# Spreading the attention output over three cycles, moving a layer norm later, and interleaving two MLP output groups in a transformer block

## The chip, the cores and the metric

The kernel runs on one core of one Trainium2 chip. The metric is the device time of one execution in microseconds (us). Times below are medians of two to four runs (seven for the kernel before in the later rounds). One trace was kept of each kernel.

## The reference

A pre-norm block: sliding-window attention (window 256, 32 heads of 32), then an MLP with SiLU, each with a residual.

```python
x = A_x                                       # [1, 2048, 1024] bf16
h  = x + attn(layernorm(x), wqkv, wo)         # 32 heads, key at most 255 positions back
h2 = h + silu(layernorm(h) @ w1) @ w2         # hidden size 3584
```

## The kernel before

The sequence is cut into four blocks of 512 rows. Attention of block `b - 1` runs woven into the projections of block `b`; attention of the last block is woven into the output projection (`wo_group`) of blocks 0 to 2. That weaving goes in cycles: three cycles (kinds A, B, C) for each of 8 head groups.

```python
def scores(b, g, kind):                       # TensorE -> sc[0], sc[1]; ScalarE exp; GpSimd masks
    ...
    for pair in range(2):
        e = e_of(b * G + g, kind, pair)
        nc.scalar.activation(out=e[:, :, lo:hi], in_=sc[pair][:, :, lo:hi], func=ACT.Exp, scale=scale)
        ...

def attn_out(b, g, pair):                     # 24 small matmuls into one bank, then divide
    for qt in range(4):
        for hh in range(2):
            ...
                nc.tensor.matmul(o_ps[:, qt * 2 + hh, 0:VW], lhsT=e_of(i, kind, pair)[...], rhs=v[...], ...)
    nc.vector.reciprocal(out=recip[:], in_=o_ps[:, :, DH:VW])
    nc.vector.tensor_tensor(out=obuf[i % 3][...], in0=o_ps[...], in1=recip[...], op=ALU.mult)

def tail_of(b, g):
    return [lambda: attn_out(b, g, 0), lambda: attn_out(b, g, 1), lambda: attn_transpose(b, g)]

# ---- last attention stage: 24 cycles, n = 0..23
for g in range(G):
    for kind in KINDS:
        scores(NB - 1, g, kind)
        b, j, c = dense[n]
        if c == 0:
            ... load_res(nb, nj, x2d)          # residual rows for the tile after this one, 256 KB
        wo_group(b, j, c)                      # 8 matmuls; VectorE adds the residual; h to DRAM
        if pending:
            pending.pop(0)()                   # a step of the tail of the head group before
        if n % 2 == 0 and n // 2 < KT:
            nc.sync.dma_start(out=w1[:, n // 2, :], ...)       # 0.9 MB
        if n == 9:
            steps = ln2_steps(0)               # load h of block 0 (1 MB), 4x statistics, 1x root,
        if n == 17:                            # 4x normalise, 4x transpose by DMA
            nc.sync.dma_start(out=w2[0], ...)
        if steps and n >= 9:
            steps.pop(0)()
        n += 1
    pending = tail_of(NB - 1, g)
```

All these transfers are issued, in program order, from one queue (SyncE's). The MLP's first group needs all four transposed tiles of LN2 (the layer norm ahead of the MLP).

The softmax here doesn't subtract the row's maximum and nothing guards it: scores larger than these inputs give would overflow.

## Time and profile before

| | kernel before |
|---|---|
| time, median of 3 runs | 720.51 us (720.36 to 721.69) |
| span of the profiled run | 718.4 us |
| TensorE busy | 695.8 us, 97% |
| VectorE, ScalarE, GpSimd busy | 41%, 36%, 24% |

The prediction shows the lines it rests on. This is the same trace cut by stage: start to the third head group; the rest of the first three attention stages; the last stage; the gap ahead of the MLP; the first MLP layer of block 0. Columns: stretch, length, busy time (instructions) of TensorE, weight loads, VectorE, ScalarE, GpSimd, then the granted clock (TensorE's, as a share of full speed), the busy share of the DMA engines and GB/s.

```profile
70.62:243.82 173.20, 169.97 (x1950) 86.68 (x1981) 84.91 (x202) 120.17 (x133) 116.29 (x253) 1.00 0.23 49
243.82:311.42 67.60, 63.49 (x757) 32.42 (x768) 35.64 (x84) 46.59 (x49) 44.89 (x98) 1.00 0.88 260
311.42:312.44 1.02, 0.00 (x1) 0.03 (x1) 0.69 (x1) 0.22 (x1) 1.02 (x4) 1.00 0.37 69
312.44:375.81 63.37, 63.04 (x330) 29.38 (x337) 25.18 (x39) 16.12 (x27) 0.34 (x1) 1.00 0.39 129
```

The last stage differs from the others in its DMA share: 0.88 against 0.23. And the chain of waits, in this stage, leaves TensorE (shortened; columns: start, length, what):

```profile
271.64 6.40 DMA r_a<-h_dram
278.13 1.30 DVE ln_st L153 x2
...
309.13 3.17 DMA r_a<-r_a
```

From the load of h at 271.64 to the first TensorE piece in the chain at 292.47 it runs through VectorE only, and at the end through the DMA transposes into the MLP.

### The profile page before, as it was taken

The numbers are of one execution on the slowest core, as the hardware profiler recorded it, in microseconds if no ns is written. First come the engines' busy times: TensorE is split into PE (matmuls) and PEld (weight loads), VectorE is DVE, ScalarE is ACT, GpSimd is POOL, SyncE is SP. The second block draws the span as 40 slices with busy tenths as digits, with TensorE's granted clock in tenths as the row PEclk, the third lists the DMA queues.
The fourth block names the chain that finished last, engine by engine and source line by source line (L and its number), as shares of the span: only waits on it lengthen the run. The fifth ranks groups of instructions, "written<-read, shape, count | busy, mean of one in ns | idle before, by whom it ended". The sixth has DMA issues, their size and how long they took to land.

```text
span 718.4 us, 12082 instructions
## 1 busy us (share of the span) xinstructions
PE 695.8 (97%) x4920; PEld 330.1 (46%) x5006; DVE 294.2 (41%) x645; ACT 257.1 (36%) x325; POOL 172.9 (24%) x375
## 2 busy tenths in 40 slices
PE   6899999999999998999999999999999999999998
PEld 2444544554455544444444444444444444444443
DVE  7355745743343436634343314325133352234111
ACT  2315556777777776641230003310023200133000
POOL 1004656766776676630000000000000000000000
PEclk9999999999999999999999999999999999999999
DMA  9440133023400388897105140012310032300010
GB/s 312 156 117 9 31 46 96 16 45 47 140 16 17 108 283 287 232 212 278 47 2 160 37 110 0 1 56 63 81 37 0 1 96 58 82 1 0 30 37 22
DMA packets 75112, 60.56 MB, mean 84 GB/s; under 512 B 48944, under 2 KB 59184, under 8 KB 75056
## 3 DMA queue, kind: packets, MB, share of 16 engines
q1 hardware_dynamic: 75056, 59.78, 29.6%
q8 instruction: 39, 0.64, 0.4%
q14 instruction: 17, 0.14, 0.1%
HBM read 39.85 MB, written 8.39 MB: 67 GB/s over the span
## 4 chain that ended last, share of the span: by engine, by line
PE 91%; DMA 3%; DVE 2%; issue 1%; ACT 1%; POOL 1%; SPq 0%; DVEq 0%; POOLq 0%; ACTq 0%
PE hacc L408 18%; PE hacc L450 17%; PE acc L206 16%; PE acc L450 9%; PE acc L408 9%; PE acc L198 8%; PE sc L234 5%; PE o_ps L270 4%; PE acc L216 4%; PE hacc L216 1%; DMA r_w<-in_A_wqkv_dram 1%; DMA r_a<-h_dram 1%; DMA r_a<-in_B_w_dram 1%; DVE ln_st L153 1%; POOL r_e L260 1%
## 5 line engine op out<-in xcount | busy, mean ns | idle before, releaser
L245 ACT ACTIVATE r_e<-sc 128x1024 bf16<-128x1024 f32 (+2 forms) x192 | 175.8, 967 | 80.0 <-PE sc L234 78.9
L260 POOL TENSOR_SCALAR_AFFINE_SELECT r_e<-r_e 128x256 bf16<-128x256 bf16 (+1 forms) x368 | 169.9, 491 | 139.2 <-ACT r_e L245 136.0
L450 PEld LDWEIGHTS <-r_a 128*128 128x128 bf16 x896 | 87.7, 98 | 106.3 <-issue 0.7
L408 PEld LDWEIGHTS <-r_w 128*128 128x128 bf16 x896 | 87.4, 98 | 106.5 <-issue 1.5
L450 PE MATMUL hacc<-r_a 128*128 128x512 bf16 x548 | 121.5, 379 | 0.6
L408 PE MATMUL hacc<-r_e,r_w 128*128 128x512 bf16 x441 | 100.1, 379 | 0.8
L417 ACT ACTIVATE r_n<-hacc 128x512 f32<-128x512 f32 x30 | 17.9, 597 | 179.5 <-PE hacc L408 128.9
L208 DVE CAST r_a<-acc 128x512 bf16<-128x512 f32 x56 | 38.7, 690 | 88.1 <-PE acc L206 88.1
L450 PE MATMUL acc<-r_a 128*128 128x512 bf16 x332 | 73.8, 379 | 0.6 <-DMA r_a<-in_B_w_dram 0.4
L206 PEld LDWEIGHTS <-r_w 128*128 128x128 bf16 x512 | 46.1, 98 | 58.6 <-issue 8.9
L206 PE MATMUL acc<-r_t,r_w 128*128 128x512 bf16 x242 | 58.5, 380 | 1.7 <-issue 1.4
L206 PE MATMUL acc<-r_w 128*128 128x512 bf16 x246 | 57.1, 380 | 0.8 <-issue 0.5
L270 PEld LDWEIGHTS <-r_e 128*128 128x128 bf16 x1440 | 45.6, 96 | 17.6 <-issue 2.7
L216 PE MATMUL acc<-r_o,r_a 128*128 128x512 bf16 x196 | 48.0, 380 | 1.9 <-DVE r_t L218 0.9
L408 PE MATMUL acc<-r_e,r_w 128*128 128x512 bf16 x216 | 49.1, 379 | 0.0
L270 PE MATMUL o_ps<-r_a,r_e 128*128 128x33 bf16 x1440 | 46.2, 178 | 2.1 <-DVE r_n L278 2.1
L234 PE MATMUL sc<-r_a 32*128 32x128 bf16 (+2 forms) x704 | 46.9, 276 | 0.3
L452 DVE SCALAR_TENSOR_TENSOR r_t<-hacc,r_t 128x512 bf16<-128x512 f32 x20 | 13.7, 684 | 61.4 <-PE hacc L450 61.2
L216 PEld LDWEIGHTS <-r_a 128*128 128x128 bf16 x256 | 23.1, 98 | 30.5 <-issue 5.9
L198 PE MATMUL acc<-r_w 128*128 128x512 bf16 x122 | 29.4, 380 | 5.0 <-ACT r_w L179 4.5
L418 DVE SCALAR_TENSOR_TENSOR r_a<-r_n,hacc 128x512 bf16<-128x512 f32 x30 | 20.6, 688 | 33.0 <-ACT r_n L417 33.0
L452 DVE SCALAR_TENSOR_TENSOR r_t<-acc,r_t 128x512 bf16<-128x512 f32 x12 | 8.3, 692 | 59.6 <-PE acc L450 59.6
(58 smaller groups left out, 429.7 us busy)
## 6 DMA issues: line engine op xcount, KB each, us to landing
r_w<-in_B_w_dram SPq DMA_DIRECT2D x8, 896.0 KB, 6.5
r_a<-in_B_w_dram SPq DMA_DIRECT2D x7, 1024.0 KB, 6.7
r_w<-in_A_wqkv_dram SPq DMA_DIRECT2D x6, 1024.0 KB, 11.9
r_o<-in_A_x_dram SPq DMA_DIRECT2D x16, 256.0 KB, 4.6
r_t<-in_A_x_dram SPq DMA_DIRECT2D x16, 256.0 KB, 3.5
h_dram<-r_t SPq DMA_DIRECT2D x16, 256.0 KB, 2.9
r_t<-h_dram SPq DMA_DIRECT2D x16, 256.0 KB, 2.8
out_dram<-r_t SPq DMA_DIRECT2D x32, 128.0 KB, 1.7
```

Source lines behind the costliest of these rows:

```text
L198: nc.tensor.matmul(acc, lhsT=lnT_b[b % 2][:, kt, j * P:(j + 1) * P], rhs=wqkv[:, kt, col0:col0 + 512], start=(kt == 0), stop=(kt == KT - 1))
L206: nc.tensor.matmul(acc, lhsT=wqkv[:, kt, col0:col0 + P], rhs=lnT_b[b % 2][:, kt, :], start=(kt == 0), stop=(kt == KT - 1))
L208: copy(out=(qT, kT)[which][b][:, g, :], in_=acc)
L216: nc.tensor.matmul(acc, lhsT=qT[b][:, g, j * P:(j + 1) * P], rhs=wo[:, g, c * 512:(c + 1) * 512], start=(g == 0), stop=(g == G - 1))
L234: nc.tensor.matmul(sc[hh // 2][:, hh % 2, ch * P:(ch + nq) * P], lhsT=kT[t // 4][r0:r0 + DH, g, (t % 4) * P:(t % 4 + 1) * P], rhs=qT[b][r0 ...
L245: nc.scalar.activation(out=e[:, :, lo:hi], in_=sc[pair][:, :, lo:hi], func=ACT.Exp, scale=scale)
L260: nc.gpsimd.affine_select(out=ap, in_=ap, pattern=[[0, 2], [0, n], [sgn, P]], compare_op=ALU.is_ge if upper else ALU.is_gt, fill=0.0, base ...
L270: nc.tensor.matmul(o_ps[:, qt * 2 + hh, 0:VW], lhsT=e_of(i, kind, pair)[:, hh, ch * P:(ch + 1) * P], rhs=v[:, b * 4 + kt, g * 4 + pair * 2 ...
L408: nc.tensor.matmul(acc, lhsT=w1[:, kt, ft * P:(ft + 1) * P], rhs=ln2T[b][:, kt, :], start=(kt == 0), stop=(kt == KT - 1))
L418: nc.vector.scalar_tensor_tensor(out=gT[:, ft, :], in0=th, scalar=1.0, in1=acc, op0=ALU.add, op1=ALU.mult)
L450: nc.tensor.matmul(acc, lhsT=gT[:, ft, j * P:(j + 1) * P], rhs=w2[ft // 4][:, ft % 4, c * 512:(c + 1) * 512], start=(ft == 0), stop=(ft == ...
L452: nc.vector.scalar_tensor_tensor(out=t_out[j % 2][:, c * 512:(c + 1) * 512], in0=acc, scalar=0.5, in1=t_in[j % 2][:, c * 512:(c + 1) * 512 ...
```

## The change

Its intent: give every cycle some output matmuls, so that ScalarE's exponentials fit in every cycle; begin LN2's VectorE work later, when its load has surely landed; and put more matmuls ahead of the first use of the last slice of w2, the second MLP weight.

```diff
-    o_ps = ps.tile([P, 8, 64], F32, name="o_ps")
-    tp_ps = ps.tile([P, 1024], BF16, name="tp_ps")
+    o_ps = [ps.tile([P, 8, 64], F32, name=f"o_ps{i}") for i in range(2)]
+    tp_ps = o_ps[1][:].rearrange("p a b -> p (a b)").bitcast(BF16)
 ...
-    def attn_out(b, g, pair):
+    def attn_out(b, g, first, last):
+        for n in range(first, last):           # 16 pieces: 8 of pair 0, 8 of pair 1
+            pair, qt, hh = n // 8, n // 2 % 4, n % 2
 ...
+            if n % 8 == 7:
+                attn_norm(i, pair)
 ...
-        return [lambda: attn_out(b, g, 0), lambda: attn_out(b, g, 1), lambda: attn_transpose(b, g)]
+        def end():
+            attn_out(b, g, 11, 16)
+            attn_transpose(b, g)
+        return [lambda: attn_out(b, g, 0, 5), lambda: attn_out(b, g, 5, 11), end]
 ...
             if n == 9:
                 steps = ln2_steps(0)
+                steps.pop(0)()
 ...
-            if steps and n >= 9:
-                steps.pop(0)()
+            for _ in range(2 if n % 3 == 0 else 1):
+                if steps and n >= 14:
+                    steps.pop(0)()
 ...
+            accs = [next_acc(), next_acc()]
+            if b == 0 and j == 0:              # MLP output: 24 + 24 matmuls, then 4 + 4
+                for c in range(2):
+                    mm2(accs[c], j, c, 0, FT - 4)
```

More of the change, by code (lines that the diff above doesn't have):

```diff
@@ L178, in ln_transpose @@
             nc.tensor.transpose(out=tp_ps[:, kt * P:(kt + 1) * P], in_=xt[:, kt * P:(kt + 1) * P], identity=ident[:])
-        copy(out=dst[:, :, j * P:(j + 1) * P], in_=tp_ps[:].rearrange("p (k q) -> p k q", q=P))
+        copy(out=dst[:, :, j * P:(j + 1) * P], in_=tp_ps.rearrange("p (k q) -> p k q", q=P))
     def ln_tiles(tag):
@@ L262, in mask, with attn_norm @@
                                 fill=0.0, base=0, channel_multiplier=-sgn)
-    def attn_out(b, g, pair):
+    def attn_out(b, g, first, last):
         i = b * G + g
-        for qt in range(4):
-            for hh in range(2):
-                chunks = [x for x in CHUNKS[qt] if b * 4 + x[0] >= 0]
-                for n, (kt, kind, ch) in enumerate(chunks):
-                    nc.tensor.matmul(
-                        o_ps[:, qt * 2 + hh, 0:VW],
-                        lhsT=e_of(i, kind, pair)[:, hh, ch * P:(ch + 1) * P],
-                        rhs=v[:, b * 4 + kt, g * 4 + pair * 2 + hh, :],
-                        start=(n == 0), stop=(n == len(chunks) - 1),
-                    )
+        for n in range(first, last):
+            pair, qt, hh = n // 8, n // 2 % 4, n % 2
+            chunks = [x for x in CHUNKS[qt] if b * 4 + x[0] >= 0]
+            for m, (kt, kind, ch) in enumerate(chunks):
+                nc.tensor.matmul(
+                    o_ps[pair][:, qt * 2 + hh, 0:VW],
+                    lhsT=e_of(i, kind, pair)[:, hh, ch * P:(ch + 1) * P],
+                    rhs=v[:, b * 4 + kt, g * 4 + pair * 2 + hh, :],
+                    start=(m == 0), stop=(m == len(chunks) - 1),
+                )
+            if n % 8 == 7:
+                attn_norm(i, pair)
+    def attn_norm(i, pair):
         recip = small.tile([P, 8, 1], F32, name="recip", tag="recip")
-        nc.vector.reciprocal(out=recip[:], in_=o_ps[:, :, DH:VW])
+        nc.vector.reciprocal(out=recip[:], in_=o_ps[pair][:, :, DH:VW])
         nc.vector.tensor_tensor(
             out=obuf[i % 3][:, :, pair * 64:(pair + 1) * 64].rearrange("p t (h d) -> p t h d", d=DH),
-            in0=o_ps[:, :, 0:DH].rearrange("p (t h) d -> p t h d", h=2),
+            in0=o_ps[pair][:, :, 0:DH].rearrange("p (t h) d -> p t h d", h=2),
             in1=recip[:].rearrange("p (t h) o -> p t h o", h=2).to_broadcast([P, 4, 2, DH]), op=ALU.mult,
@@ L443, with mm2 @@
         steps = ln2_steps(b + 1) if b + 1 < NB else []
+        def mm2(acc, j, c, first, last):
+            for ft in range(first, last):
+                nc.tensor.matmul(acc, lhsT=gT[:, ft, j * P:(j + 1) * P], rhs=w2[ft // 4][:, ft % 4, c * 512:(c + 1) * 512],
+                                 start=(ft == 0), stop=(ft == FT - 1))
         for j in range(4):
@@ L446 @@
                 load_res(b, j + 1, h_dram)
+            accs = [next_acc(), next_acc()]
+            if b == 0 and j == 0:
+                for c in range(2):
+                    mm2(accs[c], j, c, 0, FT - 4)
             for c in range(2):
-                acc = next_acc()
-                for ft in range(FT):
-                    nc.tensor.matmul(acc, lhsT=gT[:, ft, j * P:(j + 1) * P], rhs=w2[ft // 4][:, ft % 4, c * 512:(c + 1) * 512],
-                                     start=(ft == 0), stop=(ft == FT - 1))
+                acc = accs[c]
+                mm2(acc, j, c, FT - 4 if b == 0 and j == 0 else 0, FT)
                 nc.vector.scalar_tensor_tensor(out=t_out[j % 2][:, c * 512:(c + 1) * 512], in0=acc, scalar=0.5,
```

## The prediction

> **What bounds the kernel now.** I read the page's engine shares first, then the timeline of TensorE over a few attention cycles, then VectorE and the DMA-issuing queue where TensorE shows idle time.
>
> ```profile
> PE 695.8 (97%) x4920; PEld 330.1 (46%) x5006; DVE 294.2 (41%) x645; ACT 257.1 (36%) x325; POOL 172.9 (24%) x375
> ```
>
> TensorE leaves 22.6 us of the 718.4 us span unbusy, about half of it in the first 12 us. So a gain must come from the few visible gaps or from idling that the modelled matmul ends hide. The attention part (63 to 311 us) is made of cycles: scores of one kind (A, B or C) into two score tiles, one dense group of eight matmuls, then a "tail" step of the head group before: first attention output of head pair 0, then of pair 1, then only a transfer. Three cycles are a triple; a triple takes 8.02 us (A starts at 123.56, 131.58, 139.60). TensorE, then ScalarE:
>
> ```profile
> 121.40 0.40 PE L234 MATMUL sc<-r_a 32*128 32x128 bf16 x8
> 121.73 1.90 PE L198 MATMUL acc<-r_w 128*128 128x512 bf16 x8
> 123.56 0.73 PE L234 MATMUL sc<-r_a 32*128 32x384 bf16 x8
> 124.23 1.90 PE L198 MATMUL acc<-r_w 128*128 128x512 bf16 x7
> 125.97 0.76 PE L270 MATMUL o_ps<-r_a,r_e 128*128 128x33 bf16 x24
> 126.66 0.40 PE L234 MATMUL sc<-r_a 32*128 32x256 bf16 x8
> 126.99 1.90 PE L198 MATMUL acc<-r_w 128*128 128x512 bf16 x8
> 128.73 0.76 PE L270 MATMUL o_ps<-r_a,r_e 128*128 128x33 bf16 x24
> 129.42 0.40 PE L234 MATMUL sc<-r_a 32*128 32x128 bf16 x8
> ```
>
> ```profile
> 121.92 1.94 ACT L245 ACTIVATE r_e<-sc 128x1024 bf16<-128x1024 f32 x2 [0.70 <-PE sc L234]
> 124.38 1.94 ACT L245 ACTIVATE r_e<-sc 128x1024 bf16<-128x1024 f32 x2 [0.52 <-PE sc L234]
> ```
>
> Cycle lengths are uneven: C 2.16 (no output matmuls), A 3.10, B 2.76. ScalarE needs 1.94 us per cycle plus 0.52 until it can begin again, 2.46. In the 2.16 us cycle that does not fit: A's scores start at 123.56, but the second score tile is read until 121.92 + 1.94 = 123.86. A's scores hold TensorE 0.67 (to 124.23), B's and C's 0.33, for the same number of products. The 0.34 us is a wait inside a line that looks busy. So in two cycles of three TensorE bounds, in the third ScalarE.
>
> Then two places where TensorE is seen idle. VectorE stands still for the load of block 0 for the second layer norm (LN2), and the work TensorE needs queues behind:
>
> ```profile
> 278.13 1.29 DVE L153 BATCH_NORM_STATS2 ln_st<-r_a 128x6 f32<-128x512 bf16 x2 [3.62 <-DMA r_a<-h_dram]
> 279.58 0.64 DVE L218 TENSOR_TENSOR r_t<-acc,r_t 128x512 bf16<-128x512 f32 x1
> ```
>
> ```profile
> 280.26 1.89 PE L216 MATMUL acc<-r_o,r_a 128*128 128x512 bf16 x7 [0.88 <-DVE r_t L218]
> 282.87 0.77 PE L270 MATMUL o_ps<-r_a,r_e 128*128 128x33 bf16 x24 [0.72 <-DVE r_n L278]
> ```
>
> With a third wait of 1.42 at 292.5 the two triples from 275.89 take 9.84 and 9.59: 3.4 us over two normal ones. Second, the DMA queue at the end of attention:
>
> ```profile
> 307.81 2.71 SPq L175 DMA_TRANSPOSE r_a<-r_a  x2
> 312.18 0.33 SPq L221 DMA_DIRECT2D h_dram<-r_t  x1
> 312.60 1.23 SPq L286 DMA_TRANSPOSE r_a<-r_n  x1
> ```
>
> The last LN2 transpose issues about 309.1 and lands 3.2 later; the MLP starts at 312.44 after 1.02 us of idling. A transpose holds the issuing queue for 1.2 to 1.3 us, and the queue is in order.
>
> **What the Trainium skill says.** "TensorE: Matmul & The Clock Gate", section "Wait — 56ns, not 53.3ns?": 215.7 ns start to start at 512 columns and a floor near 25 ns however small the matmul. The trace agrees: 8 dense in 1.73 us (216 each); 24 output matmuls in about 0.60 (25 each). "TensorEngine Tiling (Array Packing)", "Key Properties": changing the tiling mode drains the engine. The trace shows about 0.1 us before each set of scores (dense straight into scores 1.83 against 1.73); once per cycle before and after the change. "PSUM — Partial Sum Buffer", "PSUM bank collisions raise a hardware error": two engines must be kept apart by bank. That is why the output matmuls waited for VectorE's division (0.72 above) with one bank. "TensorE: Matmul & The Clock Gate", "HAM oscillation — how this bites in real kernels": gaps over about 3.4 us re-throttle the array to half speed. No gap of the kernel before, after its start, is that long, so its trace shows nothing of it; the first 14 matmuls do run slow (4 in the first 1.5 us).
>
> **Part 1, even spread.** Nothing is removed: the 48 output matmuls of a triple become 15, 18 and 15. The cost of a cycle to TensorE is 0.33 + 1.73 + 0.10 + 0.025 x 15 = 2.53 for A and C, 2.60 for B; a triple 7.66 to 7.68 instead of 8.02. ScalarE's 2.46 fits in each, by 0.07, so the 0.34 goes and nothing takes its place. In block 0's attention (fewer chunks: 9, 13, 14) the C cycle is 2.51 and a triple 7.2 for 7.54, again 0.34. A scores that follow an output-less C cycle before and a full one after: groups 2 to 7 of the first stage (group 1 follows group 0, whose cycles have no tail) and all 8 of three later stages, 30 in all. 30 x 0.34 = **-10.3 us**. Masks on GpSimd take 5.7 us per triple, below 7.68. The second PSUM bank (the old transpose scratch, free after the start) lets pair 1 begin without waiting for pair 0's division; in steady state that wait was already hidden.
>
> **Part 2, later LN2.** The load stays at cycle 9, the statistics begin at cycle 14 instead of 10, over 10 us later; the load took 6.4. The VectorE stall for it goes. But 13 steps are pressed into 10 cycles, two in cycles 15, 18, 21. Playing VectorE forward (residual add 0.6, division pair 0.62, statistics 1.5 per tile; reciprocal root 2.9 at 135.4, 3.9 at 287.3): it falls about 4 us behind by cycle 17 and the add of cycle 18 comes about 0.9 late for the accumulator of cycle 20. So 3.4 saved, 0.9 given back: **-2.5 us**.
>
> **Part 3, the price of lateness.** The 13 steps end in cycle 23, the last, not in 22. In that cycle the queue first gets the attention transpose, which now follows the output's last five pieces in the same cycle and so waits for VectorE's division, and only then the last LN2 transpose. With the last matmul of attention ending at T: division done T + 1.0 (add 0.6, reciprocal and multiply 0.65 after the dense group), attention transpose 1.23, LN2 transpose issues T + 2.3, lands 3.2 to 3.9 later. The MLP needs all four tiles for its first group, so it starts at T + 5.6 to 6.2 instead of T + 1.0: **+4.8 us**. The gap is over 3.4 us, so I add an estimate from the clock page for half-speed restart: 3.4 us of work at half speed costs 1.7, taken at two chances in three: **+1.2 us**.
>
> **Part 4, interleaved first two MLP outputs.** Before, the last four matmuls of the first group wait 0.42 for the last slice of w2. Now 48 matmuls (10.4 us) come ahead of them, and the load takes 5.5: **-0.4 us**. The rest of the MLP is dense on TensorE and untouched.
>
> Sum: 720.5 - 10.3 - 2.5 + 4.8 + 1.2 - 0.4 = 713.3; I take **713.0 us**, 1.0% faster.
>
> **Rivals.** (a) ScalarE takes over as the bound: margin is only 0.07 us per cycle and about zero in the first stage. For it: C to A needs 2.50 measured and gets 2.51 there. Against: where it binds, it costs hundredths. If 0.1 per A is left, 3 us less gain: 716. (b) The end gap does not appear, because the transposes issue earlier than I order them, and VectorE keeps up: 720.5 - 10.3 - 3.4 - 0.4 = 706.4, just short of 2%. Against: the program order at cycle 23 is plain. (c) VectorE becomes the bound in cycles 14 to 21, by more than 0.9: residual loads also queue behind the waiting attention transposes, and one such wait of 2.57 us is in the trace before. It could eat the whole 3.4: 714. (d) Contention lengthens the last transposes; each further us is one us of time.
>
> **Range and chances.** The attention term is well measured (8.5 to 10.5), LN2 0 to 3.4, the gap 3 to 6.5, the clock 0 to 2. Together 708.5 to 717.5. Faster by over 2% needs below 706.1, lower than rival (b): 0.06. Slower by over 2%: 0.01.
>
> **What would show it.** A's scores (384-wide) should hold TensorE 0.33, triples last about 7.7, ScalarE idle before A grow by about 0.1 and before B and C shrink. VectorE's wait for the block 0 load should be gone; a small TensorE wait on the residual add near cycle 20 may be there. Before the first MLP group TensorE should wait 5 to 6 us for the last transpose, with an attention transpose just ahead of it in the queue, and the matmuls after it may run near 430 ns apart. Wrong if the triples stay near 8.0 or if that gap stays at 1 us.

## The result, and the profile after

The changed kernel took **718.06 us** (717.23 to 718.93, 4 runs) against 721.1 us for the kernel before in the same rounds (4 runs). The ratio is 0.9957, 95% interval 0.9936 to 0.9978: the same within 2%, and outside the predicted range of 708.5 to 717.5. (A ratio here is the mean time of one kernel's fast runs over that of the other's of the same rounds, so not quite the ratio of the medians.) The order of effects was largely foreseen; one of them came out with the other sign.

TensorE in the changed kernel, one cycle of kind A and the next of kind B:

```profile
122.76 0.40 PE L234 MATMUL sc<-r_a 32*128 32x384 bf16 x8
123.09 1.90 PE L198 MATMUL acc<-r_w 128*128 128x512 bf16 x8
124.83 0.53 PE L270 MATMUL o_ps<-r_a,r_e 128*128 128x33 bf16 x15
125.30 0.40 PE L234 MATMUL sc<-r_a 32*128 32x256 bf16 x8
```

A's scores (384 wide) now take 0.33 us, 122.76 to 123.09, as B's do; the hidden wait is gone. The same cut by stage as before, with one stretch more, the gap:

```profile
72.04:237.83 165.79, 164.05 (x1950) 88.08 (x1981) 84.58 (x202) 120.24 (x132) 116.27 (x253) 1.00 0.23 51
237.83:303.35 65.52, 61.00 (x759) 33.18 (x768) 35.03 (x85) 46.51 (x48) 44.85 (x97) 1.00 0.85 258
303.35:309.97 6.62, 0.06 (x4) 0.03 (x2) 0.96 (x3) 0.00 (x0) 1.04 (x3) 0.75 0.91 193
309.97:375.02 65.05, 64.51 (x329) 29.77 (x337) 25.17 (x39) 16.12 (x27) 0.00 (x0) 0.97 0.34 119
```

The first three attention stages became 7.4 us shorter. The last one, with 8 head groups where these have 22, became only 2.1 shorter. Then TensorE idles for 6.62 us, and what follows takes 1.7 us longer than before. What TensorE waits for (total, times, longest):

```profile
PE acc L417 <- DMA r_a<-r_a: 6.6, 1, 6.6
PE acc L216 <- DVE r_t L218: 3.8, 3, 1.6
```

The second line is new in size: three waits of 0.87, 1.39 and 1.57 us in the last stage for VectorE's residual add, where the kernel before had one of 0.88 for that add and two of 0.72 and 1.42 for the attention division. VectorE itself, ahead of the second:

```profile
275.63 1.29 DVE L218 TENSOR_TENSOR r_t<-acc,r_t 128x512 bf16<-128x512 f32 x2 [5.19 <-DMA r_t<-in_A_x_dram]
```

It no longer waits for h of block 0, as planned. It waits for a residual load instead, which was issued at 266.92, right after the 1 MB load of h at 266.49, and took 8.58 us. The DMA queue at the end of attention, and TensorE after it:

```profile
300.68 4.07 SPq L175 DMA_TRANSPOSE r_a<-r_a  x3
304.85 0.53 SPq L221 DMA_DIRECT2D h_dram<-r_t  x1
305.48 1.21 SPq L290 DMA_TRANSPOSE r_a<-r_n  x1
306.75 1.30 SPq L175 DMA_TRANSPOSE r_a<-r_a  x1
```

```profile
309.97 0.58 PE L417 MATMUL acc<-r_a,r_w 128*128 128x512 bf16 x1 [6.56 <-DMA r_a<-r_a]
310.77 2.76 PE L417 MATMUL acc<-r_a,r_w 128*128 128x512 bf16 x6 [0.22 <-DMA r_t<-in_A_x_dram]
```

Attention ends at 303.35; the last LN2 transpose is issued 3.4 us later, behind the attention transpose, and lands 3.2 us after that. The first MLP group then takes 3.36 us (to 313.33) instead of 1.73; the granted clock of that stretch is 0.50.

One more difference belongs to neither kernel: in this profiled run the first 16 dense matmuls of the start took 5.20 us against 3.87 in the profiled run of before, 1.3 of the 1.4 us by which the stages begin later. It is there before anything changed begins, and it is the clock: from 9.9 to 13.3 us the granted clock was 0.53 here and 1.00 in the kernel before. Three other variants (a_warm30, a_tiles, a_tiles_defer) have it too, with 0.53 to 0.55; nine have 1.00. The starts of both kernels have the same instructions, apart from the bank that the first transposes use.

### The profile page after: what moved, and what is told of

Read it like the earlier page. It is cut to its first block, busy times and chain, and to the rows that moved or that the text cites. A ratio compares the mean times of both kernels' runs of the same rounds, so it can differ in the third digit from the quotient of the medians.

```text
span 717.0 us, 12077 instructions
## 1 busy us (share of the span) xinstructions
PE 691.0 (96%) x4916; PEld 333.4 (47%) x5006; DVE 292.9 (41%) x645; ACT 257.1 (36%) x325; POOL 172.8 (24%) x375
## 4 chain that ended last, share of the span: by engine, by line
PE 91%; DMA 3%; DVE 2%; SPq 1%; ACT 1%; issue 1%; POOL 1%; DVEq 0%; POOLq 0%; ACTq 0%
PE hacc L417 18%; PE hacc L455 17%; PE acc L206 16%; PE acc L455 10%; PE acc L417 9%; PE acc L198 8%; PE o_ps L270 4%; PE sc L234 4%; PE acc L216 3%; DMA r_t<-in_A_x_dram 3%; PE hacc L216 1%; SPq L175 1%; DVE r_t L218 1%; POOL r_e L260 1%; ACT r_w L179 1%
## 5 line engine op out<-in xcount | busy, mean ns | idle before, releaser
L270 PEld LDWEIGHTS <-r_e 128*128 128x128 bf16 x1440 | 50.4, 96 | 23.0 <-issue 0.6
L206 PE MATMUL acc<-r_t,r_w 128*128 128x512 bf16 x240 | 60.0, 380 | 0.8
L206 PE MATMUL acc<-r_w 128*128 128x512 bf16 x246 | 57.7, 380 | 0.5
L270 PE MATMUL o_ps<-r_a,r_e 128*128 128x33 bf16 x1440 | 51.2, 178 | 0.0
L234 PE MATMUL sc<-r_a 32*128 32x128 bf16 (+2 forms) x704 | 37.2, 276 | 0.1
L198 PE MATMUL acc<-r_w 128*128 128x512 bf16 x122 | 31.0, 395 | 4.9 <-ACT r_w L179 4.5
```

The costliest lines, as they stand in the source:

```text
L198: nc.tensor.matmul(acc, lhsT=lnT_b[b % 2][:, kt, j * P:(j + 1) * P], rhs=wqkv[:, kt, col0:col0 + 512], start=(kt == 0), stop=(kt == KT - 1))
L206: nc.tensor.matmul(acc, lhsT=wqkv[:, kt, col0:col0 + P], rhs=lnT_b[b % 2][:, kt, :], start=(kt == 0), stop=(kt == KT - 1))
L234: nc.tensor.matmul(sc[hh // 2][:, hh % 2, ch * P:(ch + nq) * P], lhsT=kT[t // 4][r0:r0 + DH, g, (t % 4) * P:(t % 4 + 1) * P], rhs=qT[b][r0 ...
L270: nc.tensor.matmul(o_ps[pair][:, qt * 2 + hh, 0:VW], lhsT=e_of(i, kind, pair)[:, hh, ch * P:(ch + 1) * P], rhs=v[:, b * 4 + kt, g * 4 + pa ...
```

## The experiments

Theory at the outset: the score waits are gone as computed, and the gain was lost (a) because the last LN2 transpose sits in the last cycle, (b) because the late attention transpose holds the queue, so that residual loads come late. Rivals: (c) VectorE's burst of LN2 steps makes the waits; (d) the later attention transpose makes the gap. Twelve kernels ran; `before` beside them had medians of 720.7 to 720.9 us.

| kernel | median us | ratio to before (95%) | last stage, us | idle ahead of the MLP, us |
|---|---|---|---|---|
| changed kernel | 718.06 | 0.9957 (0.9936 to 0.9978) | 65.5 | 6.6 |
| e_attn_only | 717.16 | 0.9948 (0.9919 to 0.9978) | 69.7 | 3.5 |
| e_ln2_only | 726.46 | 1.0072 (1.0049 to 1.0095) | 67.6 | 5.7 |
| e_ilv_only | 721.34 | 1.0006 (0.9991 to 1.0021) | 68.9 | 1.0 |
| a_tr_defer | 715.03 | 0.9923 (0.9890 to 0.9955) | 63.5 | 5.1 |
| a_hb_10 | 718.65 | 0.9965 (0.9940 to 0.9990) | 66.5 | 6.8 |
| a_ln2_12 | 716.86 | 0.9941 (0.9926 to 0.9956) | 67.8 | 3.5 |
| a_warm | 718.50 | 0.9965 (0.9950 to 0.9980) | 66.2 | 2.5 |
| a_warm30 | 717.01 | 0.9945 (0.9929 to 0.9962) | 66.0 | under 0.3 |
| a_one_bank (2 runs) | 763.51 | 1.0592 (1.0571 to 1.0613) | 77.7 | 5.4 |
| b_tiles | 718.11 | 0.9960 (0.9945 to 0.9975) | 65.5 | 0.6 |
| a_tiles | 710.42 | 0.9852 (0.9833 to 0.9871) | 65.4 | 0.4 |
| a_tiles_defer | **706.95** | 0.9794 (0.9773 to 0.9815) | 62.3 | none |

The length of a last stage is taken in each trace from its first scores to the end of its last output matmul.

### Each part alone

**The spread and the second bank alone** (changed kernel with the LN2 lines and the interleave put back):

```diff
-                steps.pop(0)()
 ...
-            for _ in range(2 if n % 3 == 0 else 1):
-                if steps and n >= 14:
-                    steps.pop(0)()
+            if steps and n >= 9:
+                steps.pop(0)()
 ...
```

> The kernel before with the even spread and the second PSUM bank alone (LN2 of block 0 one step per cycle from cycle 9 as before, no interleave). Theory: the 30 hidden score waits of 0.34 us go, and the last LN2 transpose is again issued in cycle 22, so the gap ahead of the MLP is 2 us or less and no matmul runs at half clock; the wait of about 0.9 us near the second cycle of the last attention stage (residual loads behind the late attention transpose) is here too, and the old LN2 stall of about 3.4. Time 711 to 713. Rival, that the later attention transpose makes the gap: a gap of 4 us or more here too, time 716 or more.

Measured 717.16 us: a miss by 4 to 6 us, and the most useful one. The 30 score waits are gone (first three stages as in the changed kernel), but the last stage is 69.7 us, longer than the 67.6 of the kernel before. VectorE and TensorE in it:

```profile
273.83 1.29 DVE L153 BATCH_NORM_STATS2 ln_st<-r_a 128x6 f32<-128x512 bf16 x2 [6.86 <-DMA r_a<-h_dram]
```

```profile
275.97 3.57 PE L216 MATMUL acc<-r_o,r_a 128*128 128x512 bf16 x8 [4.47 <-DVE r_t L218]
```

Counted from the start of the stage, TensorE reaches cycle 10 a little sooner than in the kernel before (34.7 us against 35.2), but the load of h is issued later (29.1 against 27.8) and takes longer (8.3 us against 6.4). VectorE waits 6.86 us instead of 3.62, TensorE 4.47, and the eight matmuls after it take 3.57 us, that is at half clock. The gap ahead of the MLP is 3.5 us, although the last transpose is issued in cycle 22. This trace is of the slowest of the four runs (719.89 us; the others took 716.4 to 717.2, and where they were shorter is not known). But the medians point the same way: about 10 us of score waits are gone, and the time is 3.6 us shorter. So neither (a) nor (b) nor (d) is the whole cause: **in the last stage TensorE was not the only bound.** I read it so: the LN2 chain (h to DRAM, 1 MB load, statistics, root, normalisation, four transposes) takes about as long as the stage did, and a shorter stage on TensorE turns work into waiting.

**The later LN2 alone** (kernel before with the two LN2 hunks of the change):

> The kernel before with the later LN2 alone (load in cycle 9, other steps from cycle 14, two in cycles 15, 18, 21). Theory: the gap ahead of the MLP comes from the place of the last LN2 transpose in cycle 23, so it is 5 to 6 us here too, with the old attention order, and the first matmuls after it run at half clock: 723 to 726, slower than before. Rival, that the gap comes from the attention transpose waiting for the spread-out output: gap below 3 us, time 717 to 720.

Measured 726.46 us, slower than before, as the theory said. The gap is 5.67 us with the old attention order, because this is what the queue does at the end:

```profile
312.01 0.33 SPq L221 DMA_DIRECT2D h_dram<-r_t  x1
312.43 1.23 SPq L286 DMA_TRANSPOSE r_a<-r_n  x1
313.71 1.30 SPq L175 DMA_TRANSPOSE r_a<-r_a  x1
```

So most of the gap comes from the place in cycle 23, and rival (d) falls as its whole cause; deferring the attention transpose (below) takes 1.5 of 6.6 us. The half clock is here too (3.36 us for the first group). And the stage itself is 67.6 us, no shorter than before: the wait for h has gone, but the doubled steps make TensorE wait 1.65 us for VectorE's division in cycle 19, and cycle 20 then takes 3.33 us instead of 2.16, with eight dense matmuls in 3.0 us and a granted clock of 0.70 over the 3.9 us after the wait:

```profile
299.06 0.77 PE L270 MATMUL o_ps<-r_a,r_e 128*128 128x33 bf16 x24 [1.65 <-DVE r_n L278]
300.09 3.06 PE L216 MATMUL acc<-r_o,r_a 128*128 128x512 bf16 x8
```

In this trace moving LN2 later saved nothing even by itself.

**The interleave alone** (kernel before with the `accs` and `mm2` lines of the change):

> The kernel before with the interleaved first two MLP output groups alone. Theory: TensorE's 0.42 us wait for the last slice of w2 goes and nothing else moves: 0.3 to 0.7 us shorter, which the start-up scatter of about 1.5 us between runs may hide in the times; the trace decides.

Ratio 1.0006: nothing in the times. In the trace the wait for the w2 slice is gone and the first two groups follow each other without a gap:

```profile
382.02 5.34 PE L446 MATMUL hacc<-r_a 128*128 128x512 bf16 x24
387.20 1.03 PE L446 MATMUL acc<-r_a 128*128 128x512 bf16 x4
```

The gain is real (in the changed kernel the rest of the MLP is 0.6 us shorter, see the end) and below the scatter of the times. This run shows one source of scatter: with the code of the last stage unchanged, the stage took 68.9 us here and 67.6 in the trace of before. The cycle that waits for h took 6.65 us instead of 4.58, because TensorE's wait in it was 2.40 us and the eight matmuls after it took 3.32, at half clock; with 0.88 us in the trace of before they did not.

### What holds the residual loads

**Attention transposes one cycle later** (changed kernel; the queue gets each of them after the next cycle's loads, when the division is long done):

```diff
         def end():
             attn_out(b, g, 11, 16)
-            attn_transpose(b, g)
+            late.append((b, g))               # issued at the next group's first tail step
 ...
```

> The changed kernel with each attention transpose issued one cycle later, after that cycle's loads, so that the queue no longer stands still for VectorE's division. Theory: the 0.9 us wait at the start of the last stage goes, the 1.4 us wait for the residual load behind the LN2 load shrinks below 0.7, the gap shrinks by about 1.3 to 5.3 or less: 713 to 715.5. Rival, that VectorE's own burst of LN2 steps makes all three waits: the waits stay within 0.5 us of 0.9, 1.4 and 1.6, and the time is 716.5 or more.

Measured 715.03 us, within the expected range. The waits of 0.9 and 1.4 us are gone; 2.0 us in two waits remain in cycles 18 to 20, which are VectorE's backlog after the burst; the gap is 5.1 us:

```profile
PE acc L429 <- DMA r_a<-r_a: 5.1, 1, 5.1
PE acc L216 <- DVE r_t L218: 2.0, 2, 1.4
```

So (b) made the first two waits and (c) the third: both are right, for different waits. The trace is of the fastest of four runs that spread from 713.3 to 717.3, so from the times alone the 3.0 us below the changed kernel are not sure.

**The load of h one cycle later, after that cycle's residual load:**

```diff
-            if n == 9:
+            if n == 10:
                 steps = ln2_steps(0)
```

> The changed kernel with the 1 MB LN2 load issued in cycle 10, after that cycle's residual load, instead of cycle 9 ahead of it. Theory: the residual load no longer queues behind it, lands in 5 us or less instead of 8.6, and the 1.4 us wait for it is below 0.5; waits at the start and in cycle 20 stay; 716 to 717.5. Rival, that the w1 loads or VectorE cause that wait: it stays at 1 us or more, time as the changed kernel, 718.

Measured 718.65 us, no gain: a miss. The wait in cycle 14 is gone, and a larger one stands in cycle 15:

```profile
279.59 0.69 DVE L218 TENSOR_TENSOR r_t<-acc,r_t 128x512 bf16<-128x512 f32 x1 [5.66 <-DMA r_t<-in_A_x_dram]
```

The residual load after it, issued at 270.18, takes 9.4 us. In both orders the residual load issued within 5 us behind h was late (8.6 and 9.4 us); changing their places only chose which.

**LN2 begun two cycles sooner:**

```diff
-                if steps and n >= 14:
+                if steps and n >= 12:
```

> The changed kernel with the LN2 steps begun in cycle 12 instead of 14 (same doubling), so that the last transpose is issued in cycle 21. Theory that the fixed length of the LN2 chain (store, 1 MB load, statistics, normalisation, four transposes) now sets the end of the stage, and that its start matters as much as its last cycle: gap 2 to 4 us instead of 6.6, VectorE's wait in cycles 12 to 14 grows by about 1, time 714 to 716. Rival, that only the queue position of the last transpose counts: gap 1 us or less, no other wait grows, time 710 to 711.5.

Measured 716.86 us. The gap falls to 3.5 us as the chain theory said, and the cost comes out within the stage, 67.8 us, more than the 1 us expected: in cycle 18, which takes 6.32 us, TensorE waits 2.11 us for VectorE's backlog, and the granted clock of the 3.4 us after that is 0.52. The rival, that only the queue position counts, falls.

### The half clock after the gap

**20 idle matmuls inside the gap** (results thrown away; output unchanged):

```diff
+    for i in range(20):
+        nc.tensor.matmul(sc[0][:, i % 2, :], lhsT=w1[:, 0, 0:P], rhs=w1[:, 0, 0:512], start=True, stop=True)
     ps_sc.__exit__(None, None, None)
```

> The changed kernel with 20 idle matmuls (about 4.3 us at full clock, results thrown away) behind the last attention output, that is inside the gap of 6.6 us. Clock theory: the gap to the first MLP matmul keeps its end (the last transpose lands when it did), but the eight matmuls after it run at about 216 ns and not 430, so the granted clock of that stretch is 1.00 instead of 0.50 and the run is 1.3 to 1.7 us shorter. Rival, that the slow matmuls wait for weights or for the transfer and not for the clock: they stay slow and the time stays.

A miss: 718.50 us, and the group after the gap still took 3.3 us. The matmuls end at 306.9 and 2.50 us of idling are left. TensorE, and the stretch after the gap:

```profile
309.44 3.46 PE L419 MATMUL acc<-r_a,r_w 128*128 128x512 bf16 x8 [2.50 <-DMA r_a<-r_a]
```

```profile
310.00:313.00 3.00, 3.00 (x17) 1.19 (x16) 0.00 (x0) 0.00 (x0) 0.00 (x0) 0.50 0.80 253
```

The granted clock is 0.50, so it is the clock; it only needed less idling than the 3.4 us I had counted with. **30 of them**, which fill the gap:

> As a_warm with 30 matmuls (6.5 us), which fill the gap to within 0.5 us. There 20 of them left 2.5 us of idling and the matmuls after it still ran at half clock, so that miss left the clock theory open. Clock theory, with any idling of about 2.5 us being enough: the first eight MLP matmuls now take 1.7 to 1.8 us and not 3.3, granted clock 1.00 there, run 1.2 to 1.7 us shorter than the changed kernel. Rival (weights or transfers slow them): they stay at 3.2 us or more, time as the changed kernel.

The group takes 1.74 us (310.38 to 312.12) and the clock stays up:

```profile
309.10:311.00 1.90, 1.77 (x9) 0.61 (x8) 0.00 (x0) 0.00 (x0) 0.00 (x0) 1.00 0.96 200
```

Time 717.01 us, 1.0 below the changed kernel; the trace's 1.6 us are partly covered by the scatter of the start. The clock theory stands. Across the traces, from the attention stages on, TensorE waits of up to 1.57 us were followed by full clock. Those of 1.65, 2.05, 2.11, 2.40, 2.50 (two) and 2.55 us were followed by half clock, and so were all above 3.5; those of 1.85, 2.18, 2.24 and 2.34 by full clock again. (The 2.05, 2.18, 2.24, 2.34, 2.55 and one 2.50 are in a_one_bank, below.) So between 1.6 and 2.6 us it went either way.

### The second bank

**One bank for both pairs:**

```diff
-    o_ps = [ps.tile([P, 8, 64], F32, name=f"o_ps{i}") for i in range(2)]
+    o_ps = [ps.tile([P, 8, 64], F32, name="o_ps0")] * 2
```

> The changed kernel with one PSUM bank for both pairs (the scratch for transposes separate again). Theory, that the even spread needs the second bank: in every B cycle the first output matmul of pair 1 follows the last of pair 0 at once and waits for VectorE to divide it out, 0.9 to 1.3 us in each of 31 triples; 740 to 760. Rival, that the second bank is only convenience: below 725.

763.51 us, a little over the expected range, and the waits are where they were expected:

```profile
PE o_ps L270 <- DVE r_n L282: 43.0, 32, 2.6
```

1.3 us each in 32 places. The even spread needs the second tile. Whether it must lie in another bank is not tested: here, as in the kernel before, both pairs also write the same elements, so the second pair has to wait for the first one's division in any case.

### LN2 tile by tile

If the LN2 chain is the cause, it has to be taken apart and not shifted. The rows of block 0's tile `j` are sent to DRAM in cycle 2j + 1 (the edit is shortened here):

```diff
+            for step in ln2.get(n, []):        # cycle 2j+3: 256 KB load of tile j; 2j+5: its statistics;
+                step()                         # 12: root; 13+j: normalise; 17+j: transpose
-            if n == 9: ... steps = ln2_steps(0) ...
```

With the deferred attention transposes:

> The changed kernel with the deferred attention transposes and LN2 of block 0 taken tile by tile: four 256 KB loads in cycles 3, 5, 7, 9 in place of one of 1 MB, statistics in 5 to 11, reciprocal root in 12, normalisation in 13 to 16, transposes in 17 to 20, never two in a cycle. Theory that the LN2 chain is what ate the gain: no TensorE wait above 0.5 us in the last stage, gap below 1 us, no half clock, time 705 to 708.5. Rival, that the DMA engines are simply full in the last stage: residual loads are late again, waits of 1 us or more, time above 710.

706.95 us, in the expected range and the best of all. The last stage and the start of the MLP:

```profile
237.99:300.28 62.29, 61.34 (x772) 32.87 (x770) 34.94 (x84) 46.51 (x48) 44.76 (x97) 1.00 0.97 281
```

```profile
299.90 0.53 PE L270 MATMUL o_ps<-r_a,r_e 128*128 128x33 bf16 x15
300.28 1.89 PE L438 MATMUL acc<-r_a,r_w 128*128 128x512 bf16 x8
```

No gap and no half clock. One wait of 0.94 us is left in cycle 15, after the reciprocal root, so the expected "none above 0.5" was not quite met. TensorE is busy for 61.34 of the 62.29 us, so little more is to be had in this stage from waits. The DMA share is now 0.97; VectorE still waits 6.2 us in all for residual loads, but it no longer passes these waits on to TensorE. By its own sign (above 710 us) the rival, that the DMA engines are simply full, falls.

Without the deferral:

> a_tiles_defer without the deferred attention transposes. Theory that the late attention transposes hold the loads behind them: TensorE waits of 1 to 3 us in all in the last stage (0.9 at its start among them), time 708 to 711, slower than a_tiles_defer by 1 to 4. Rival, that only the LN2 chain mattered: no wait above 0.5 beyond the one of 0.9 in cycle 15, time within 1 us of a_tiles_defer.

710.42 us; waits of 3.8 us in four places:

```profile
PE acc L216 <- DVE r_t L218: 3.8, 4, 1.5
```

The stage is as long as in the changed kernel (65.4 us against 65.5), so here the tiles gained by the gap and the half clock that are gone, not within the stage. The deferral is worth 3.5 us on its own, so the held queue mattered beside the LN2 chain. The tiles also put the statistics and transposes into earlier cycles; no run parts the splitting of the load from this new schedule. And the kernel before with this LN2 alone:

> The kernel before with that tile-by-tile LN2 alone. Theory: the old stall of 3.4 us and the gap of 1.0 go and nothing else, since the score waits stay: 716 to 717.5. Rival (DMA engines full): 718.5 or more.

718.11 us, 2.6 below before where 4 had been expected: waits of about 0.3, 0.9 and 0.6 us stay. From b_tiles to a_tiles_defer, which is the spread, the deferral and the interleave with LN2 out of the way, it is 11.2 us: what the prediction's parts 1 and 4 promised together (10.7).

## Why the prediction was wrong

By its own steps, from the two cuts by stage (spans 718.4 and 717.0):

| step | predicted, us | measured, us | from |
|---|---|---|---|
| score waits, 30 x 0.34 | -10.3 | -10.2 | 173.20 to 165.79, and 8 triples of 8.02 to 7.67 in the last stage |
| later LN2 | -2.5 | +0.7 | last stage beyond its triples: 3.44 before, 4.16 after |
| gap ahead of the MLP | +4.8 | +5.6 | 1.02 to 6.62 |
| half clock after it | +1.2 | +1.7 | 63.37 to 65.05 |
| interleave | -0.4 | -0.6 | rest of the MLP, 342.59 to 341.98 |
| sum | -7.2 | -2.8 | medians: 721.1 to 718.06, -3.0 |

- **Part 1 was right** to a tenth of a microsecond: the wait hidden in A's scores, the 30 places, and that ScalarE's 2.46 us just fit. Only its "nothing takes its place" failed in the last stage: the attention transpose, now behind the spread output, brought the wait of 0.87 us at the start, which the table has under LN2.
- **The step that failed is Part 2**, "So 3.4 saved, 0.9 given back". The wait for h went as said, 3.4 us. In its place stand 3.8 us of waits, not 0.9. Under it lay a second one: the residual load behind the same 1 MB, hidden as long as VectorE stood still for h (1.39 us). In front of it a third came up, because the attention transpose now waits for the division and holds every load behind it (0.87 us at the start of the stage). And the backlog cost 1.57, not 0.9. With the transposes deferred the first two are gone. With the later LN2 alone the stage was 67.6 us, as before, and a stage of unchanged code varies by 1.3, so +0.7 is no sure loss: the step's own gain is nil. Rival (c) had named the mechanism, the residual loads behind waiting transposes. But its 714 does not follow: without the step's 2.5 the prediction's own sum is 715.8.
- **Part 3 had the mechanism and the sign**; its size was 0.8 short, because the three transposes ahead ended at T + 1.4 and not before T + 1.0, after a late residual load had delayed the store ahead of them. Its clock term was 0.5 short because it was taken at two chances in three; the full estimate of 1.7 came. The mechanism was right: the granted clock was 0.50 over the 3.3 us after the gap.
- **What the prediction overlooked as a whole**: it treated the last stage as a stage of TensorE with a few accidents. The chain of waits of the kernel before ran through LN2 and its DMA, and the DMA share there was 0.88. The spread alone (717.16) shows it: with 2.8 us fewer of score waits in that stage, its trace has the stage 2.1 us longer.
- **Slips in its working.** Of TensorE's 22.6 us of idling 4.6 lie in the first 12 us and 8.1 in the first 30, not half in the first 12. Two thirds of 1.7 is 1.1, not 1.2. The terms' own ranges add up to 709.2 to 720.1, so the stated 717.5 was narrower on the slow side. And the output matmuls before the change waited not only because of the bank: both pairs wrote the same elements.
- In the result, the LN2 hunk is the right idea in the wrong cycles: with the spread in place it replaces a 4.47 us wait by three smaller ones and a gap, so the two parts together are about as good as the spread alone.

What stays open: why the load of h took 6.4 us before and 8.3 in the spread-only run. Chance has a part, since with unchanged code in that stage e_ilv_only shows 7.9. More w1 traffic close ahead is likely (in a_tr_defer, with no w1 load issued in the 6.9 us ahead of it, it took 5.5), and was not tested apart. Open too is why the clock falls at the start in some runs.

## What to carry to other kernels

Before you shorten a stage on its busiest engine, ask which chain crosses the stage from end to end (here store, load, statistics, transposes): it does not get shorter, and waits that were hidden come up. A wait that ended with a transfer may hide another behind the same transfer, so removing the wait is not removing the transfer; four tiles of 256 KB, loaded as they became ready and with their steps spread out, were worth more here than any shift of the 1 MB. On an in-order queue, an item that waits for compute holds all loads behind it: issue it a cycle later, when its input is surely done. And a TensorE wait of about 2 us may cost nearly double: up to 1.7 us of half clock came after such waits here.

## What the Trainium skill lacked or had wrong

- "TensorE: Matmul & The Clock Gate", section "HAM oscillation — how this bites in real kernels", puts the idle gap that brings the half clock at about 3.4 us. Here waits of 1.65, 2.05, 2.11, 2.40, 2.50 and 2.55 us were enough: the eight dense matmuls after them took 2.7 to 3.3 us instead of 1.73. Waits of 1.85, 2.18, 2.24 and 2.34 us brought none, so there is no sharp limit in these runs. Above it the page and the runs agree: all waits over 3.5 us were followed by half clock.
- "DMA: Bandwidth & Descriptors", section "Issuing engines are not separate DMA queues", calls the sequencer's time to start a DMA usually small relative to the DMA itself. For the DMA transposes here it was 1.2 to 1.3 us of the queue against 3.2 us to landing, and up to 2.45 us. Of the gap of 6.62 us ahead of the MLP, the first 3.4 passed before the last of five transposes in the queue was issued.
